# A fused attention and gated-MLP kernel: feature exponential taken straight from K and Q, some PSUM chunks emptied by VectorE, one weight block loaded later

## The chip, the cores and the metric

The kernel runs on one core of a Trainium2 chip. The metric is the device time of one execution in microseconds; before the change the median of three runs is 350.18 us (346.5 to 350.24). The core has five engines that run side by side, each with its own in-order queue: TensorE (PE, matmuls; its weight loads are shown as PEld), VectorE (DVE), ScalarE (ACT), GpSimd (POOL) and SyncE (SP, which here only issues DMAs). [...]

## What is computed

The input x is 2048 x 640 in bf16. It is layer-normed; the normed xn goes through an attention over four segments of 512 rows with a recurrent memory, and through a gated MLP, and the result is x + attention * silu(MLP). Cut to what matters:

```python
phi = lambda t: jnp.where(t > 0, t + 1.0, jnp.exp(t))
for s in range(4):                                  # segments of 512 rows, 32 heads of 20
    qs, ks, vs = q[:, :, s], k[:, :, s], v[:, :, s]
    p = softmax(einsum('bhqd,bhkd->bhqk', qs, ks) * scale + mask)
    a_dot = einsum('bhqk,bhkd->bhqd', p, vs)
    num = einsum('bhld,bhde->bhle', phi(qs), M)
    den = einsum('bhld,bhd->bhl', phi(qs), z)[..., None] + 1e-06
    o = g * num / den + (1.0 - g) * a_dot
    M = M + einsum('bhld,bhle->bhde', phi(ks), vs)
    z = z + phi(ks).sum(over l)
attn = o @ wo
mlp = (sigmoid(xn @ w_gate) * (xn @ w_up)) @ w_down   # 640 -> 1536 -> 640
out = x + attn * silu(mlp)
```

The feature map phi is t + 1 for positive t and exp(t) otherwise. It is applied to every K and Q of a segment that the memory reads or is updated with.

## The kernel before

**Tiles.** A segment is 512 rows. K and Q are kept transposed, 640 features as five chunks of 128 partitions x 512 columns in one tile (`k5`, `q5`); V is kept by rows, with a column of ones. The MLP's hidden 1536 features are 12 blocks of 128. Gate and up weights lie in three tiles each (`Wg[0..2]`, `Wu[0..2]`), four blocks of 128 columns to a tile; a load of one such tile moves 640 KB (`load_glu`, L161 to L163).

**Slots.** The scores of a segment are worked off in 20 slots (4 pairs of head groups, 5 units each). A slot begins with four or eight groups of score matmuls into the single score buffer `Sps` (L526), one softmax exponential on ScalarE over all of it (L531, into `pt`), and a mask on GpSimd (L534). The probabilities of the slot before are multiplied with V in `weigh` (L551). Between these, TensorE gets other work: V tiles, K chunks and Q chunks of the next segment, memory reads and updates, the output projection, and the MLP as filler (`gate`, `up`, `down`).

**Order.** The order of instructions on each engine is decided while the program is built. Tasks have a due time and a planned cost (`at(time, cost, fn, ...)`, L103); times are in slots, and many are multiples of R = 20/24. Tasks with a cost over 0.1 count as TensorE work (`tasks`), the others are `soft`. Each slot has two halves: up to 0.45 of the slot only `tasks` are taken, then comes `weigh`, then the rest with `tasks` and `soft`. The flag `delay` is true in the first half. The MLP's blocks fill the slots up to a common level, which is worked out from the planned costs of the tasks (L700 to L705). `later(lag, fn)` puts a soft task `lag` times R slots after the time at which the current one was due.

**Steps around the change.**
- `k_chunk` (L282), `q_chunk` (L314) and `v_tile` (L356) run five matmuls into one of three PSUM buffers that all of this work shares (`dtile`, L114), and empty it: K (L291) and V (L364) by ScalarE, Q by ScalarE in segment 0 and by VectorE in the others (`evacuate`, L276 to L280).
- `phi` (L367) handles a chunk of K or Q, 30 chunks in all: on VectorE min(t, 0) into `mn` (L370) and t + 1 in place (L371); 0.8 R later exp on ScalarE (L374); 0.5 R later the maximum of the two on VectorE (L378). For K a DMA transpose into `pkt` is issued by SP 0.7 R after that (L382).
- `k5` has one buffer, so the first K chunk of the next segment can only be emptied into it when the transposes of the segment before have read it.
- `q_bound` (L329) multiplies |Q| with the maxima of |K|: the bound that keeps the softmax exponential in range. ScalarE copies it to `cb` (L337), SP writes it to DRAM (`c_out`, L345) and reads it back as extra rows of Q (`c_in`, L353), without which a segment's scores can't start. For segments 1 to 3 it is due at 19.2 R with a planned cost of 1.12 (L660).
- At the start (`startup`, L577) nothing of the slots runs yet. Q goes to DRAM in two pieces (`stage_out`, L310), comes back in head order (`relay`, L274), the bound goes out and comes back, and SP issues all of these in program order. The second gate tile's load, `load_glu(1, 0)`, is issued after the first piece of Q (L609); the gate of block 4, the first that needs it, is the second piece of MLP work inside the slots.

Of the kernel before, what the change touches and what calls it, by code (L numbers as in the profile page):

```python
# [9 lines left out]
P = 128  # L10
# [3 lines left out]
DH = 20  # L14
# [3 lines left out]
L = 512  # L18
# [8 lines left out]
BF = mybir.dt.bfloat16  # L27
F32 = mybir.dt.float32
U16 = mybir.dt.uint16
ACT = mybir.ActivationFunctionType  # L30
ALU = mybir.AluOpType
# [24 lines left out]
R = NSLOT / 24  # L56
# [3 lines left out]
def kernel(  # L60
# [14 lines left out]
    nc = tc.nc  # L75
# [9 lines left out]
    stg = ctx.enter_context(tc.tile_pool(name="stg", bufs=1))  # L85
# [17 lines left out]
    def at(time, cost, fn, *a):  # L103
        count[0] += 1
        heapq.heappush(tasks if cost > 0.1 else soft, (time, count[0], cost, fn, a))

    seq = [0]
    delay = [False]
# [16 lines left out]
    def later(lag, fn, *a):  # L125
        at(clock[0] + lag * R, 0.0, fn, *a)
# [34 lines left out]
    def load_glu(i, which):  # L161
        w, src = ((Wg, B_w_gate), (Wu, B_w_up))[which]
        nc.sync.dma_start(w[i][:], src[:, i * L:(i + 1) * L].rearrange("(c p) n -> p c n", p=P))  # L163
# [19 lines left out]
    for i in range(8):  # L183
        va = cpool.tile([P, H, VW], BF, name=f"va{i}")
# [83 lines left out]
    def half_tile(tiles, n, half):  # L268
        return tiles[(2 * n + half) % 3]
# [3 lines left out]
        for r in range(4):  # L273
            nc.sync.dma_start(half_tile(dst, n, half)[32 * r:32 * r + DH, :, :], rows[r][:, 4 * half:4 * half + 4, :])  # L274

    def evacuate(n, dst, ps):  # L276
        if n == 0:
            nc.scalar.copy(dst, ps)
        else:
            nc.vector.tensor_copy(dst, ps)  # L280

    def k_chunk(n, c):  # L282
        s = st[n]
        if c == 0:
            s["k5"] = stg.tile([P, DC, L], BF, name="k5")
            s["kabs"] = stg.tile([P, DC], F32, name="kabs")
        ps = dtile([P, L], F32, "psk")
        for k in range(DC):
            nc.tensor.matmul(ps[:], lhsT=W["k"][:, k, c * P:(c + 1) * P], rhs=s["xnT"][:, k, :],  # L289
                             start=(k == 0), stop=(k == DC - 1))  # L290
        nc.scalar.copy(s["k5"][:, c, :], ps[:])  # L291
        if c in (2, 4) and n:
            later(0.9, stage_out, n, c // 4, Ks, KT, "k5")
        if n:
            later(0.7, k_max, n, c)
        else:
            k_max(n, c)
# [16 lines left out]
    def q_chunk(n, c):  # L314
        s = st[n]
        if c == 0:
            s["q5"] = stg.tile([P, DC, L], BF, name="q5")
            s["aq"] = stg.tile([P, DC, L], BF, name="aq")
        ps = dtile([P, L], F32, "psq")
        for k in range(DC):  # L320
            nc.tensor.matmul(ps[:], lhsT=W["q"][:, k, c * P:(c + 1) * P], rhs=s["xnT"][:, k, :],  # L321
                             start=(k == 0), stop=(k == DC - 1))
        evacuate(n, s["q5"][:, c, :], ps[:])
        nc.vector.tensor_scalar(s["aq"][:, c, :].bitcast(U16), s["q5"][:, c, :].bitcast(U16), 0x7FFF, None,
                                op0=ALU.bitwise_and)
        if c in (2, 4) and n:
            later(0.9, stage_out, n, c // 4, Qs, QT, "q5")
# [21 lines left out]
    def c_in(n, halves=(0, 1)):  # L349
        rows = Cs[n % 2].rearrange("b (g r) n -> r b g n", r=4)  # L350
        for half in halves:
            for r in range(4):
                nc.sync.dma_start(half_tile(QT, n, half)[32 * r + DH:32 * r + KR, :, :],  # L353
                                  rows[r][:, 4 * half:4 * half + 4, :])

    def v_tile(n, j, half):  # L356
        s = st[n]
        ps = dtile([P, HB], F32, "psv")
        for k in range(DC):
            nc.tensor.matmul(ps[:], lhsT=s["xnT"][:, k, j * P:(j + 1) * P],  # L360
                             rhs=W["v"][:, k, half * HB:(half + 1) * HB],
                             start=(k == 0), stop=(k == DC - 1))
        va = V[4 * (n % 2) + j]
        nc.scalar.copy(va[:, half * 16:(half + 1) * 16, 0:DH], ps[:].rearrange("p (h e) -> p h e", e=DH))  # L364


    def phi(n, src, c):  # L367
        t = st[n][src][:, c, :]
        mn = stg.tile([P, L], BF, name="mn", bufs=2)
        nc.vector.tensor_scalar(mn[:], t, 0.0, None, op0=ALU.min)  # L370
        nc.vector.tensor_scalar(t, t, 1.0, None, op0=ALU.add)  # L371

        def exp():
            nc.scalar.activation(mn[:], mn[:], ACT.Exp)  # L374
            later(0.5, rest)

        def rest():
            nc.vector.tensor_tensor(t, t, mn[:], op=ALU.max)  # L378
            if src == "k5":
                if c == 0:  # L380
                    st[n]["pkt"] = stg.tile([P, 4, D], BF, name="pkt")
                later(0.7, lambda: nc.sync.dma_start_transpose(st[n]["pkt"][:, :, c * P:(c + 1) * P], t))  # L382
        later(0.8, exp)


    def m_update(n, cs):
# [190 lines left out]
    def startup():  # L577
        warm(WARM)
        nc.gpsimd.memset(KT[0][:], 1.0)
        ln_stats(0, 0, 0, 1)  # L580
        ln_stats(0, 0, 1, 2)
        ln_norm(0, 0, 0)
        warm(10)
        ln_stats(0, 1, 0, 1)
        ln_norm(0, 0, 1)
        v_tile(0, 0, 0)
        ln_stats(0, 1, 1, 2)
        v_tile(0, 1, 0)
        ln_norm(0, 1, 0)
        v_tile(0, 0, 1)  # L590
        ln_norm(0, 1, 1)
        v_tile(0, 2, 0)
        v_tile(0, 1, 1)
        v_tile(0, 2, 1)
        v_ones(0, 4)
        make_ind()
        nc.gpsimd.memset(KT[1][:], 1.0)
        for c in range(DC):
            k_chunk(0, c)
        nc.gpsimd.memset(KT[2][:], 1.0)  # L600
        stage_out(0, 0, Ks, KT, "k5")
        for c in range(DC):
            q_chunk(0, c)
            if c == 0:
                stage_out(0, 1, Ks, KT, "k5")
                relay(0, 0, Ks, KT)
            elif c == 2:
                stage_out(0, 0, Qs, QT, "q5")
                load_glu(1, 0)  # L609
            if c < 2:  # L610
                ln_stats(1, 0, c, c + 1)
        make_bd()
        v_ones(4, 8)
        v_tile(0, 3, 0)
        v_tile(0, 3, 1)
        relay(0, 0, Qs, QT)
        q_bound(0)
        stage_out(0, 1, Qs, QT, "q5")
        c_in(0, (0,))
        load_glu(1, 1)  # L620
        ln_stats(1, 1, 0, 1)
        take(1)
        gates()
        take(1)
        ln_norm(1, 0, 0)
        ln_norm(1, 0, 1)
        take(1)
        ln_stats(1, 1, 1, 2)
        take(4)
        at(R * 2.0, 0.0, ln_norm, 1, 1, 0)  # L630
        at(R * 2.3, 0.0, ln_norm, 1, 1, 1)
        load_glu(2, 0)
        load_glu(2, 1)
        relay(0, 1, Ks, KT)
        relay(0, 1, Qs, QT)
        c_in(0, (1,))
# [6 lines left out]
    for n in range(NSEG):  # L643
        w = NSLOT * n
        m = n + 1
        if m < NSEG:
            if n:
                for p in range(2):
                    for i in range(2):
                        at(w + R * (1.4 * p + 0.7 * i - 3.4), 0.1, ln_stats, m, p, i, i + 1)  # L650
                        at(w + R * (0.4 + 1.6 * p + 0.4 * i), 0.1, ln_norm, m, p, i)
            for i in range(8):
                at(w + R * (3.5 + (0.6 * i if i < 4 else 2.5 + 0.55 * (i - 4))), 0.68, v_tile, m, i // 2, i % 2)
            for c in range(DC):
                at(w + R * (8.8 + 1.0 * c), 1.08, k_chunk, m, c)
                at(w + R * (13.8 + 1.1 * c), 1.08, q_chunk, m, c)
                if m + 1 < NSEG:
                    at(w + R * (12.8 + 0.85 * c), 0.0, phi, m, "k5", c)
                at(w + R * (18.3 + 0.8 * c), 0.0, phi, m, "q5", c)
            at(w + R * 19.2, 1.12, q_bound, m)  # L660
            if m + 1 < NSEG:
                for p in range(2):
                    at(w + R * (16.1 + p), 0.0, x_load, m + 1, p)
            if n == 0:
                for c in range(DC):
                    at(R * (2.6 + 0.8 * c), 0.0, phi, 0, "k5", c)
            for i, cs in enumerate(([0, 1, 2], [3, 4])):
                at(w + R * (10.0 + 3.2 * i), 0.75 - 0.25 * i, m_update, n, cs)
        if n >= 1:
            for j in range(4):  # L670
                at(w + R * (1.1 + 0.3 * j), 0.0, o_ready, n - 1, j)
                at(w + R * (4.0 + 0.5 * j if j < 3 else 9.6), 0.0, xr_load, n - 1, j)
            for i in range(8):
                at(w + R * (5.4 + 1.1 * i), 0.68, o_proj, n - 1, i // 2, i % 2)
                at(w + R * (3.4 + 0.85 * i), 0.25, mem_read, n, i // 2, i % 2)
# [72 lines left out]
    n = NSEG - 1  # L748
# [39 lines left out]
```

## Time and profile before

| What | Value |
|---|---|
| time, median of three runs | 350.18 us |
| the profiled execution | 350.39 us |
| its span, first to last instruction | 348.3 us |
| mean granted TensorE clock | 0.988 |
| chain that ended last | PE 79%, DVE 7%, ACT 6%, DMA 5%, issue 2% |
| softmax exponential, L531 | 80 of 1.88 us, 150.1 us |
| feature exponential, L374 | 30 of 0.63 us |
| minimum, add, maximum, L370, L371, L378 | 30 each of 0.31, 0.32 and 0.49 us |
| K and V chunks emptied by ScalarE, L291 and L364 | 20 of 0.585 us and 32 of 0.434 us |
| Q chunks emptied by VectorE, L280 | 15 of 0.687 us |

The busy share of an engine is an average over the whole span. For this kernel, in which TensorE is busy 96% of the time, a change is worth what it takes away of the time in which TensorE waits or runs at a lower clock; an engine off that path may get faster or slower without any effect. All times that follow are microseconds from the start of the span unless they are durations.

### The profile page before, as it was taken

What the parts mean: (1) busy time and instruction counts of PE and PEld (TensorE: products, weight loads), DVE (VectorE), ACT (ScalarE), POOL (GpSimd) and SP (SyncE); (2) the same over time, 40 slices, a digit from 0 to 9 for tenths busy, and PEclk for the clock granted to TensorE, in tenths of its full rate; (3) what the DMA queues carried; (4) which work ended last, traced back from release to release, by engine and by line L of the source; (5) the groups of instructions that cost most, each with busy time, mean ns of one, the idle gap of its engine ahead of it and who ended that gap; (6) DMA issues with size and microseconds to landing.
All of it is one profiled execution on the core that took longest, in us unless ns stands there. A gap on an engine that the chain in (4) does not pass through costs nothing.

```text
span 348.3 us, 8395 instructions
## 1 busy us (share of the span) xinstructions
PE 333.0 (96%) x3402; PEld 187.4 (54%) x3402; DVE 215.1 (62%) x541; ACT 233.8 (67%) x258; POOL 111.0 (32%) x157
## 2 busy tenths in 40 slices
PE   7998999899898999999989999999999999999995
PEld 7543355454455456554456446654446655544673
DVE  5365354369839456789759766685565577633455
ACT  3652589778659676667667678666678776687730
POOL 6554222222226222323214422333232322232214
PEclk9999899999989999999999999999999999999999
DMA  7955986664950641034641172123220431020032
GB/s 251 329 184 152 260 130 79 219 177 101 181 124 1 96 115 38 21 101 116 171 107 34 39 115 77 38 91 102 86 87 13 58 96 38 31 86 3 2 60 75
DMA packets 54725, 35.53 MB, mean 102 GB/s; under 512 B 28576, under 2 KB 54688, under 8 KB 54688
## 3 DMA queue, kind: packets, MB, share of 16 engines
q1 hardware_dynamic: 52480, 32.23, 37.7%
q10 hardware_dynamic: 2208, 2.79, 2.6%
q8 instruction: 26, 0.43, 0.5%
q14 instruction: 11, 0.09, 0.1%
HBM read 20.19 MB, written 8.39 MB: 82 GB/s over the span
## 4 chain that ended last, share of the span: by engine, by line
PE 79%; DVE 7%; ACT 6%; DMA 5%; issue 2%; SPq 0%; ACTq 0%; DVEq 0%
PE gp L432 13%; PE up L442 13%; PE yp L460 13%; PE Aps L551 8%; PE Sps L526 7%; PE psq L321 6%; PE sp L506 6%; PE psk L289 6%; PE psv L360 5%; ACT pt L531 3%; DMA pkt<-k 2%; DMA Cs<-cb 1%; PE dm L392 1%; PE am L414 1%; DMA Qs<-q 1%
## 5 line engine op out<-in xcount | busy, mean ns | idle before, releaser
L531 ACT ACTIVATE pt<-Sps 128x2048 bf16<-128x2048 f32 x80 | 150.1, 1876 | 20.5 <-PE Sps L526 19.8
L534 POOL TENSOR_SCALAR_AFFINE_SELECT pt<-pt 128x1024 bf16<-128x1024 bf16 (+1 forms) x80 | 75.8, 947 | 204.0 <-ACT pt L531 204.0
L432 PE MATMUL gp<-xnT,Wg 128*128 128x512 bf16 x240 | 60.7, 384 | 0.5 <-DVE hT L446 0.4
L442 PE MATMUL up<-xnT,Wu 128*128 128x512 bf16 x240 | 60.1, 381 | 0.0
L460 PE MATMUL yp<-Wd,hT 128*128 128x320 bf16 x384 | 58.7, 304 | 0.4 <-DVE hT L446 0.4
L446 DVE SCALAR_TENSOR_TENSOR hT<-tg,up 128x512 bf16<-128x512 bf16 x48 | 32.7, 681 | 32.7 <-PE up L442 28.8
L551 PEld LDWEIGHTS <-pt 128*128 128x128 bf16 x1280 | 43.2, 96 | 13.9 <-issue 1.7
L435 ACT ACTIVATE tg<-gp 128x512 bf16<-128x512 f32 x48 | 28.7, 599 | 32.6 <-PE gp L432 29.9
L551 PE MATMUL Aps<-va,pt 128*128 128x21 bf16 x1280 | 44.6, 173 | 0.2 <-DVE od L560 0.2
L460 PEld LDWEIGHTS <-hT 128*128 128x128 bf16 x384 | 35.7, 99 | 15.9 <-issue 2.2
L526 PE MATMUL Sps<-QT,KT 24*128 24x128 bf16 (+3 forms) x512 | 33.0, 302 | 6.8 <-ACT pt L531 4.9
L442 PEld LDWEIGHTS <-Wu 128*128 128x128 bf16 x240 | 21.2, 97 | 22.9 <-issue 2.3
L432 PEld LDWEIGHTS <-Wg 128*128 128x128 bf16 x240 | 21.0, 98 | 22.9 <-issue 3.9
L465 DVE SCALAR_TENSOR_TENSOR aa<-t,yp 128x320 bf16<-128x320 bf16 x32 | 15.3, 482 | 24.5 <-ACT t L463 24.4
L526 PEld LDWEIGHTS <-KT 24*128 24x128 bf16 x512 | 10.1, 92 | 34.0 <-issue 32.7
L360 PE MATMUL psv<-Wv,xnT 128*128 128x320 bf16 x160 | 26.5, 299 | 0.7 <-ACT tg L435 0.5
L463 ACT ACTIVATE t<-yp 128x320 bf16<-128x320 f32 x32 | 13.7, 438 | 18.9 <-PE yp L460 17.7
L506 PE MATMUL sp<-Wo,oT 128*128 128x320 bf16 x160 | 25.9, 300 | 0.0
L289 PE MATMUL psk<-xnT,Wk 128*128 128x512 bf16 x100 | 24.2, 379 | 1.0 <-ACT k L291 1.0
L321 PE MATMUL psq<-xnT,Wq 128*128 128x512 bf16 x100 | 24.3, 380 | 0.0
L374 ACT ACTIVATE mn<-mn 128x512 bf16<-128x512 bf16 x30 | 18.9, 633 | 7.4 <-DVE mn L370 7.4
L508 DVE SCALAR_TENSOR_TENSOR aa<-aa,sp 128x320 bf16<-128x320 bf16 x32 | 15.5, 485 | 10.6 <-PE sp L506 10.4
(73 smaller groups left out, 325.7 us busy)
## 6 DMA issues: line engine op xcount, KB each, us to landing
KT<-Ks SPq DMA_DIRECT2D x32, 80.0 KB
QT<-Qs SPq DMA_DIRECT2D x32, 80.0 KB
xr<-in_A_x_dram SPq DMA_DIRECT2D x15, 160.0 KB
out_dram<-xr SPq DMA_DIRECT2D x15, 160.0 KB
xt<-in_A_x_dram SPq DMA_DIRECT2D x6, 320.0 KB
Wg<-in_B_w_gate_dram SPq DMA_DIRECT2D x3, 640.0 KB
Wu<-in_B_w_up_dram SPq DMA_DIRECT2D x3, 640.0 KB
Wd<-in_B_w_down_dram ACTq DMA_DIRECT2D x1, 1920.0 KB
```

The source lines that it names most:

```text
L289: nc.tensor.matmul(ps[:], lhsT=W["k"][:, k, c * P:(c + 1) * P], rhs=s["xnT"][:, k, :], start=(k == 0), stop=(k == DC - 1))
L321: nc.tensor.matmul(ps[:], lhsT=W["q"][:, k, c * P:(c + 1) * P], rhs=s["xnT"][:, k, :], start=(k == 0), stop=(k == DC - 1))
L360: nc.tensor.matmul(ps[:], lhsT=s["xnT"][:, k, j * P:(j + 1) * P], rhs=W["v"][:, k, half * HB:(half + 1) * HB], start=(k == 0), stop=(k == ...
L432: nc.tensor.matmul(gp[:], lhsT=Wg[f // 4][:, k, fo:fo + P], rhs=s["xnT"][:, k, :], start=(k == 0), stop=(k == DC - 1))
L442: nc.tensor.matmul(ps[:], lhsT=Wu[f // 4][:, k, fo:fo + P], rhs=s["xnT"][:, k, :], start=(k == 0), stop=(k == DC - 1))
L446: empty(lambda: nc.vector.scalar_tensor_tensor(out=h[:], in0=tg[:], scalar=1.0, in1=ps[:], op0=ALU.add, op1=ALU.mult))
L460: nc.tensor.matmul(yp[:], lhsT=s["hT"][f][:, j * P:(j + 1) * P], rhs=W["d"][:, f, hs], start=(f == 0), stop=(f == FC - 1))
L506: nc.tensor.matmul(sp[:], lhsT=s["oT"][:, j, c, :], rhs=W["o"][:, c, hs], start=(c == 0), stop=(c == DC - 1))
L526: nc.tensor.matmul(Sps[:, r, c0:c0 + ncol], lhsT=kt[32 * r:32 * r + KR, gi, kb * P:(kb + 1) * P], rhs=qt[32 * r:32 * r + KR, gi, kb * P:L] ...
L531: nc.scalar.activation(pt[:], Sps[:], ACT.Exp, scale=SCALE)
L534: nc.gpsimd.affine_select(out=diag, in_=diag, compare_op=ALU.is_ge, fill=0.0, base=0, pattern=[[0, 4], [0, cnt], [1, P]], channel_multipli ...
L551: nc.tensor.matmul(A[:, qb, r, :], lhsT=pt[:, r, off:off + P], rhs=V[4 * (n % 2) + kb][:, 4 * g + r, :], start=first, stop=True, skip_grou ...
```

## The change

It has four parts.

1. `phi` takes the exponential straight from the K or Q chunk into a tile `ex`, at the time at which the minimum and the add stood. 0.8 R later VectorE adds 1 in place and takes max(min(ex, 1), t + 1) in one scalar_tensor_tensor. Since exp(t) is at least 1 just where t is positive, and t + 1 is then larger than 1, the result is the same function.
2. `evacuate` no longer goes by segment but by the half of the slot: with `delay` set VectorE empties the chunk, otherwise ScalarE. K chunks and V tiles use it; Q chunks stay where they were.
3. The load of the second gate tile is issued behind the first half of `c_in` of segment 0.
4. `q_bound` of segments 1 to 3 is due at 19.0 R with a planned cost of 0.6.

```diff
-    def evacuate(n, dst, ps):
-        if n == 0:
+    def evacuate(dst, ps):
+        if delay[0]:
+            nc.vector.tensor_copy(dst, ps)
+        else:
             nc.scalar.copy(dst, ps)
-        else:
-            nc.vector.tensor_copy(dst, ps)
...
-        nc.scalar.copy(s["k5"][:, c, :], ps[:])
+        evacuate(s["k5"][:, c, :], ps[:])
...
-        evacuate(n, s["q5"][:, c, :], ps[:])
+        (nc.vector.tensor_copy if n else nc.scalar.copy)(s["q5"][:, c, :], ps[:])
...
-        nc.scalar.copy(va[:, half * 16:(half + 1) * 16, 0:DH], ps[:].rearrange("p (h e) -> p h e", e=DH))
+        evacuate(va[:, half * 16:(half + 1) * 16, 0:DH], ps[:].rearrange("p (h e) -> p h e", e=DH))
...
         t = st[n][src][:, c, :]
-        mn = stg.tile([P, L], BF, name="mn", bufs=2)
-        nc.vector.tensor_scalar(mn[:], t, 0.0, None, op0=ALU.min)
-        nc.vector.tensor_scalar(t, t, 1.0, None, op0=ALU.add)
-
-        def exp():
-            nc.scalar.activation(mn[:], mn[:], ACT.Exp)
-            later(0.5, rest)
+        ex = stg.tile([P, L], BF, name="ex", bufs=2)
+        nc.scalar.activation(ex[:], t, ACT.Exp)
 
         def rest():
-            nc.vector.tensor_tensor(t, t, mn[:], op=ALU.max)
+            nc.vector.tensor_scalar(t, t, 1.0, None, op0=ALU.add)
+            nc.vector.scalar_tensor_tensor(out=t, in0=ex[:], scalar=1.0, in1=t, op0=ALU.min, op1=ALU.max)
...
-        later(0.8, exp)
+        later(0.8, rest)
...
             elif c == 2:
                 stage_out(0, 0, Qs, QT, "q5")
-                load_glu(1, 0)
...
         c_in(0, (0,))
+        load_glu(1, 0)
         load_glu(1, 1)
...
-            at(w + R * 19.2, 1.12, q_bound, m)
+            at(w + R * 19.0, 0.6, q_bound, m)
```

In the built program nine K chunks and twelve V tiles move from ScalarE to VectorE; GpSimd's order is the same, and TensorE's differs only by groups that change places around the bound and in the slots before it.

## The prediction, made before the changed kernel ran

> **What bounds the kernel now.** I read the page first, for which engine is full, then the waits by who waited for whom, then the chain in order of time without its TensorE pieces, then windows around the places that stood out, and the timeline of the worst of them. Page, rows on engines and clock:
>
> ```profile
> PE 333.0 (96%) x3402; PEld 187.4 (54%) x3402; DVE 215.1 (62%) x541; ACT 233.8 (67%) x258; POOL 111.0 (32%) x157
> ...
> PEclk9999899999989999999999999999999999999999
> ```
>
> PE is busy nearly everywhere, and two slices of 8.7 us show a lower clock. ScalarE and VectorE have room on average, so work moved between them gains nothing by itself; only time in which PE waits, or runs at half speed, can be won. Waits, engine waiting <- releaser, us in total, times, longest:
>
> ```profile
> ACT mn L374 <- DVE mn L370: 7.4, 7, 1.5
> ...
> PE Sps L526 <- ACT pt L531: 4.9, 4, 2.4
> ...
> ACT k L291 <- DMA pkt<-k: 2.5, 1, 2.5
> ...
> PE Sps L526 <- DMA QT<-Cs: 1.7, 2, 1.2
> ...
> PE psk L289 <- ACT k L291: 1.0, 1, 1.0
> ```
>
> The chain in order of time (start, us, what) names what lies behind them:
>
> ```profile
> 22.81 3.31 DMA Qs<-q
> 27.68 4.33 DMA Cs<-cb
> 32.33 2.51 DMA QT<-Cs
> ...
> 58.46 6.39 DMA pkt<-k
> ```
>
> Start-up: the first scores wait for the bound's rows, and PE's row of the up block that follows starts at 35.77 where the gate block before ended near 32.81; without the 0.40 that four score matmuls take, 2.6 us are lost. Then windows (us, PE, PEld, DVE, ACT, POOL busy, PEclk, DMA share, GB/s):
>
> ```profile
> 33.04:36.45 3.41, 1.91 (x8) 0.60 (x8) 0.00 (x0) 0.99 (x2) 0.00 (x0) 1.00 0.53 125
> 36.45:39.87 3.42, 3.42 (x16) 0.96 (x14) 0.69 (x1) 1.55 (x2) 0.68 (x1) 0.50 1.28 198
> 64.40:67.80 3.40, 2.40 (x29) 1.68 (x26) 1.40 (x3) 2.84 (x4) 0.00 (x0) 1.00 0.65 210
> 94.48:97.89 3.41, 1.39 (x16) 0.91 (x16) 1.22 (x5) 3.41 (x5) 1.10 (x1) 1.00 0.87 207
> 97.89:101.31 3.42, 3.42 (x30) 2.10 (x28) 0.93 (x2) 1.76 (x2) 1.10 (x1) 0.50 0.43 127
> ```
>
> A stretch of 3.4 us with PE busy 1.91 or 1.39 is followed by one at clock 0.50; one with 2.40 is not. Each half-speed stretch costs half of 3.42, 1.7 us. The stall in front of the second one, on the timeline (start, us, what, idle before):
>
> ```profile
> 94.05 0.63 ACT L374 ACTIVATE mn<-mn 128x512 bf16<-128x512 bf16 x1 [0.82 <-DVE mn L370]
> ...
> 94.59 1.86 ACT L531 ACTIVATE pt<-Sps 128x2048 bf16<-128x2048 f32 x1
> ...
> 96.50 0.40 PE L526 MATMUL Sps<-QT,KT 24*128 24x256 bf16 x8 [2.43 <-ACT pt L531]
> ```
>
> The scores were ready near 93.0, but ScalarE is in order: the feature exponential stood first in its queue and waited for VectorE's minimum, the softmax exponential began 1.5 us late, and the next scores waited for it, there being one score buffer. What can be won is 4.9 + 1.0 + 2.6 + 2 x 1.7 = 11.9 us.
>
> **The change, part by part.**
>
> *Exponential straight from K and Q.* 30 chunks. Removed on VectorE: minimum (0.35 for k, 0.27 for q) and maximum (0.43, 0.54); the add (0.36, 0.29) stays; added: one scalar_tensor_tensor, 128x512, all bf16 in SBUF, which before does not show. Lower bound the maximum of k, 0.43, upper bound the same operation with one operand in PSUM, 0.68 (L446); I take 0.6, nearer to the same operation. Per chunk 1.12 becomes about 0.92, in all 33.6 becomes 28 us (22.6 to 30.1). None of it is on PE's path. ScalarE's work is the same (0.63 each), but its input is now a chunk emptied slots before, so the 7.4 us of waits have no source any more. Behind those waits the softmax exponentials stood, and behind them PE's 4.9 us. What is late next: at 92.96 PE multiplies the bound and its copy cb (0.58) and, in the new order, one exponential (0.63) stand before the following softmax exponential (1.87). That is 3.2 us from the end of the bound with its semaphore, against 2.4 of PE's work (scores 0.3, down block 1.64, Aps 0.4): 0.8 us stays. Of the other three waits (0.89, 0.73, 0.83) I leave 0.2. So 4.9 becomes 1.0: -3.9.
>
> The finishing step is due 0.8 after the exponential where it was 1.3 after the minimum, so the transposes of the first K features go out earlier by half a unit of R = 20/24 slot; 80 slots in 313 us make a slot 3.9, so some 1.6 us. The last was issued at 58.46, 0.23 before the 1.9 MB load of Wd, and took 6.39; the trace has the one at 56.55 landing after 2.4. Ahead of Wd it should take about 2.4, and land some 4 us earlier than 64.86, before the K chunk that overwrites its source is ready to be emptied. That wait held ScalarE 2.5 and PE 1.0: -1.0. If the transpose is not earlier, the 1.0 stays and VectorE is blocked in ScalarE's place.
>
> *First-half chunks on VectorE.* By the new order 9 K and 12 V chunks move: ScalarE loses 9 x 0.585 + 12 x 0.434 = 10.5, VectorE gains 9 x 0.687 (L280) + 12 x 0.49 (the 128x320 rows from PSUM) = 12.1. VectorE 215.1 - 5.6 + 12.1 = 222 us, 64%; ScalarE 223. In a first half the softmax exponential of 1.9 us stands before the chunk on ScalarE; VectorE frees the buffer sooner, or later, if an hT step (0.68) is before it. Per chunk -0.2 to +0.3 on PE, of which three PSUM buffers hide most; sum -1 to +3, and I take +0.7, as VectorE is over 90% busy in a few slices.
>
> *Second gate block's load.* On SP it is moved past four Q relays, the bound's write, the second half of Q and four bound reads; its own issue is 0.49. By the trace's landing records its 640 KB (issued 23.25) landed at 30.03, the relays (issued 26.1 to 27.2) between 30.4 and 31.8 and the bound's write at 32.01. Four K relays with less before them landed 2.3 to 2.7 after issue; so the Q relays by about 29.9, the bound's write about 30.2, the reads 1.8 earlier. PE's 2.6 becomes 0.8. But the block now leaves near 31.5, and the next load of this size (33.36) took 4.5: it lands near 36.0, where gate block 4 wants it at 35.1: 0.9 back, and the up block behind it 0.6. Against that the half-speed stretch is gone if PE is idle in smaller pieces; then the up block 4 starts near 38.0 instead of 39.99. This lead meets the next limit: segment 1's last xnT transposes land at 51.6 and 52.1, the V tile that wants them started at 53.62, and DMA is full in between, so they will not be earlier. The lead shrinks to 1.7. I count start-up with its half-speed stretch at -1.7 (0 to -2.5), not at 2.6 + 1.7.
>
> *Bound earlier and cheaper in the plan.* Due 16.0 slots becomes 15.83, the second half of the slot before; planned cost 1.12 becomes 0.6, which is what five of its matmuls take (0.60 at 92.96). No instruction is added; down, gate and up blocks change places with neighbours. It puts a down block into the slot that had only bound and Aps between two score groups, which is part of the 3.9. New wait: the bound follows the last Q chunk by 1.5 to 2.0 us of PE work; emptying and absolute value take 0.69 + 0.29 and semaphores 0.2. With one hT step before them PE waits 0.4, in two segments: +0.3 on average.
>
> *The second half-speed stretch* goes with the stall before it (0.8 instead of 2.4 leaves PE over 2.40 busy): -1.7. [...]
>
> Sum: -3.9 - 1.0 + 0.7 - 1.7 + 0.3 - 1.7 = -7.3; some small waits with the same causes (PE on ScalarE's tg and on VectorE's hT, 1.3 together) I count at -0.7. So -8.0 from the profiled 350.39 (span 348.3 and 2.1 around it), 342.4; it lies 0.2 over the median 350.18, hence 342.2 in the medians' terms.
>
> **Rivals.**
> 1. *The waits move.* With the minimum gone, ScalarE's own queue (exponentials, cb, chunks of second halves) is late instead: it was busy 3.41 of 3.41 in the window at 94.48. Then half of the 3.9 and the second clock stretch stay: 342.2 + 2.0 + 1.7 = 345.9. Against it: ScalarE loses 10.5 us of work.
> [...]
> 3. *The load move gives nothing*: the block lands as late as it did behind a full queue (6.8 after issue, at 38.3), gate block 4 waits 3.2 and the lead is gone: 343.9.
> 4. *Slower*: each of the 21 chunks stands behind an hT step on VectorE (0.68) and holds its PSUM buffer, so that PE waits for it. 21 x 0.68 = 14.3 gives 342.2 - 0.7 + 14.3 = 355.8; it decides from 0.42 each. Against it: 15 Q chunks are emptied there now, and no row has PE waiting for them.
>
> **Numbers.** Forecast 0.52 (own range 339 to 344.5), rival 1 0.18, rival 2 0.12, rival 3 0.07, rival 4 0.05; 0.06 that more is won, up to all of 11.9 (338). Range 337.5 to 347: the gain of all waits at its lower end, rival 1 with a full +3 for VectorE short of its upper. A measurement here tells about 2%, 7.0 us, from no change, so faster means under 343.2: about 0.7 of the forecast, a quarter of rivals 2 and 3, a tenth of 1, all of 0.06, sum 0.50. Slower by 2% (over 357.2) only in the worst of rival 4: 0.03.
>
> **What would show it.** No ScalarE wait for VectorE before the feature exponential; PE's waits on pt near 1 us; no half-speed slice near 98; the bound's reads issued near 30.2 and the second gate block as the next wait near 35; the last K transpose landing before 61; VectorE near 222, ScalarE near 223 us. Wrong: a row of PE waiting for psk, psv on VectorE, or a scalar_tensor_tensor over 0.7.

## The result and the profile after

| | before | after |
|---|---|---|
| median of 20 runs each, taken side by side, us | 348.39 (346.29 to 351.31) | 344.28 (343.5 to 348.72) |
| ratio | | 0.9884, 95% interval [0.9858, 0.991] |
| profiled execution, us | 350.39 (span 348.3, clock 0.988) | 343.56 (span 341.8, clock 0.998) |

The change makes the kernel 1.2% faster. The forecast was 342.2 us (range 337.5 to 347). The page of the changed kernel, busy time by engine and the clock by slices:

```profile
PE 326.5 (96%) x3360; PEld 187.0 (55%) x3402; DVE 223.9 (66%) x532; ACT 225.6 (66%) x237; POOL 111.2 (33%) x157
...
PEclk9999999999999999999999999999999999999999
```

No slice has a lower clock any more, and work has moved from ScalarE to VectorE (in the records 42 of the 3402 matmuls are missing, so PE's sum is not comparable with before). The waits (engine waiting <- releaser, us in total, times, longest):

```profile
PE Sps L522 <- ACT pt L527: 4.5, 7, 1.4
...
ACT ex L370 <- DVE k L374: 3.2, 2, 2.2
...
ACT ex L370 <- DVE q L374: 2.0, 2, 1.0
...
PEld L428 <- DMA Wg<-in_B_w_gate_dram: 0.8, 1, 0.8
...
PEld L438 <- DMA Wu<-in_B_w_up_dram: 0.7, 1, 0.7
```

What the reader is to see: ScalarE's wait for the minimum (7.4) and TensorE's wait for the bound's rows (1.7) are gone, and so is ScalarE's wait for the transposes of K (2.5). But TensorE's wait for the softmax exponential is 4.5 where it was 4.9, in seven pieces instead of four, and the feature exponential waits again for VectorE, now for 5.2 us. The transfers in the chain, in order of time (start, us, what):

```profile
22.06 3.17 DMA Qs<-q
26.77 2.56 DMA Cs<-cb
31.13 5.76 DMA Wu<-in_B_w_up_dram
```

The write of the bound takes 2.56 instead of 4.33, and in place of the read of its rows the chain now runs through a weight load. On the timeline, the place where TensorE's longest wait arises (start, us, what, idle before):

```profile
50.73 0.69 DVE L442 SCALAR_TENSOR_TENSOR hT<-tg,up 128x512 bf16<-128x512 bf16 x1 [2.05 <-PE up L438]
...
51.66 0.69 DVE L374 SCALAR_TENSOR_TENSOR k<-ex,k 128x512 bf16<-128x512 bf16 x1
...
52.44 0.63 ACT L370 ACTIVATE ex<-k 128x512 bf16<-128x512 bf16 x1 [2.20 <-DVE k L374]
...
52.98 1.86 ACT L527 ACTIVATE pt<-Sps 128x2048 bf16<-128x2048 f32 x1
...
54.89 0.40 PE L522 MATMUL Sps<-QT,KT 24*128 24x128 bf16 x8 [1.39 <-ACT pt L527]
```

Read from the bottom: the scores wait 1.39 for the softmax exponential, which could have begun near 51 (the scores before it started at 50.56 and take 0.40) but stands behind a feature exponential. That one has its input, a K chunk emptied long before, but not its output: `ex` has two buffers, and the older one is held until the finishing step of its chunk has read it (51.66 to 52.35). That step stands on VectorE behind an hT step which waited 2.05 for TensorE's up block. It is before's pattern with another cause. Three more waits of 1.0 (79.93, 98.76 and 179.35) have the same releaser, and behind the last two TensorE waits 0.56 each:

```profile
98.76 0.63 ACT L370 ACTIVATE ex<-q 128x512 bf16<-128x512 bf16 x1 [1.02 <-DVE q L374]
...
101.21 0.40 PE L522 MATMUL Sps<-QT,KT 24*128 24x128 bf16 x8 [0.56 <-ACT pt L527]
```

So 1.39 + 0.56 + 0.56 = 2.5 of the 4.5 follow an exponential that waited for its buffer. The four other pieces (0.25, 0.70, 0.51 and 0.54) follow ScalarE's own work: 0.51 at 92.57 stands behind the copy of the bound and one exponential, 0.70 at 85.47 behind the copy of a down block (`t`) and one exponential.

How far the clock enters is seen over the runs. The runs of before that were taken beside the experiments, grouped by the mean granted clock of each run (one stretch of half speed, 3.41 us in the profiled before, takes 1.7 us, 0.5% of the span, from the mean), and after's 20, which were taken at another time:

| granted clock | before, runs | before, median us | after, runs | after, median us |
|---|---|---|---|---|
| 0.997 or more | 8 | 346.5 | 18 | 344.25 |
| 0.992 to 0.995 | 45 | 348.7 | 0 | |
| 0.990 or less | 20 | 350.8 | 2 | 348.5 |

At full clock the gain is some 2.2 us; the rest of the 4.1 us in the medians goes with runs at a lower mean clock, of which the changed kernel has 2 in 20 and before 65 in 73. The profiled execution of before belongs to the last group.

### The profile page after: what moved, and what is told of

Read it like the earlier page. It is cut to its first block, busy times and chain, and to the rows that moved or that the text cites. A ratio compares the mean times of both kernels' runs of the same rounds, so it can differ in the third digit from the quotient of the medians.

```text
span 341.8 us, 8316 instructions
## 1 busy us (share of the span) xinstructions
PE 326.5 (96%) x3360; PEld 187.0 (55%) x3402; DVE 223.9 (66%) x532; ACT 225.6 (66%) x237; POOL 111.2 (33%) x157
## 4 chain that ended last, share of the span: by engine, by line
PE 80%; DVE 6%; ACT 5%; DMA 4%; issue 3%; SPq 1%; POOL 1%; DVEq 0%; ACTq 0%
PE up L438 14%; PE gp L428 13%; PE yp L456 13%; PE Aps L547 8%; PE Sps L522 7%; PE psk L289 6%; PE sp L502 6%; PE psq L321 6%; PE psv L360 5%; ACT pt L527 3%; DMA Wu<-in_B_w_up_dram 2%; PE dm L388 1%; PE am L410 1%; DMA Qs<-q 1%; DVE hT L442 1%
## 5 line engine op out<-in xcount | busy, mean ns | idle before, releaser
L428 PE MATMUL gp<-xnT,Wg 128*128 128x512 bf16 x222 | 58.5, 379 | 1.8 <-DVE hT L442 0.4
L438 PE MATMUL up<-xnT,Wu 128*128 128x512 bf16 x229 | 58.9, 379 | 1.1 <-DMA Wu<-in_B_w_up_dram 0.6
L456 PE MATMUL yp<-Wd,hT 128*128 128x320 bf16 x384 | 57.1, 299 | 0.0
L522 PE MATMUL Sps<-QT,KT 24*128 24x128 bf16 (+3 forms) x512 | 31.7, 300 | 4.7 <-ACT pt L527 4.5
L289 PE MATMUL psk<-xnT,Wk 128*128 128x512 bf16 x92 | 23.5, 379 | 0.4
L502 PEld LDWEIGHTS <-oT 128*128 128x128 bf16 x160 | 14.5, 98 | 8.1 <-issue 2.0
```

What stands on the lines that cost most here:

```text
L428: nc.tensor.matmul(gp[:], lhsT=Wg[f // 4][:, k, fo:fo + P], rhs=s["xnT"][:, k, :], start=(k == 0), stop=(k == DC - 1))
L438: nc.tensor.matmul(ps[:], lhsT=Wu[f // 4][:, k, fo:fo + P], rhs=s["xnT"][:, k, :], start=(k == 0), stop=(k == DC - 1))
L456: nc.tensor.matmul(yp[:], lhsT=s["hT"][f][:, j * P:(j + 1) * P], rhs=W["d"][:, f, hs], start=(f == 0), stop=(f == FC - 1))
L502: nc.tensor.matmul(sp[:], lhsT=s["oT"][:, j, c, :], rhs=W["o"][:, c, hs], start=(c == 0), stop=(c == DC - 1))
L522: nc.tensor.matmul(Sps[:, r, c0:c0 + ncol], lhsT=kt[32 * r:32 * r + KR, gi, kb * P:(kb + 1) * P], rhs=qt[32 * r:32 * r + KR, gi, kb * P:L] ...
```

## The experiments

The theory after the result: the parts work as predicted, and what is missing is the wait for a buffer of `ex`. Its rivals: ScalarE's own queue, with exponentials back to back, holds the scores; or the worth sits elsewhere (the load, the chunks), and a lead at one place is absorbed by the next limit. Where an expectation names theories by letters, they are its own. All ratios are to runs of the kernel before that were taken beside the experiment; the line numbers of these kernels are those of before outside `phi`.

### The four parts alone

**The exponential alone** (phi_alone):

```diff
-        mn = stg.tile([P, L], BF, name="mn", bufs=2)
-        nc.vector.tensor_scalar(mn[:], t, 0.0, None, op0=ALU.min)
+        ex = stg.tile([P, L], BF, name="ex", bufs=2)
+        nc.scalar.activation(ex[:], t, ACT.Exp)
...
-            nc.vector.tensor_tensor(t, t, mn[:], op=ALU.max)
+            nc.vector.tensor_scalar(t, t, 1.0, None, op0=ALU.add)
+            nc.vector.scalar_tensor_tensor(out=t, in0=ex[:], scalar=1.0, in1=t, op0=ALU.min, op1=ALU.max)
```

> The kernel before with the new feature exponential alone. Theory A (each part is worth the TensorE waits that it removes; the exponential now waits for one of its two ex buffers instead of the minimum): ScalarE's wait for mn (7.4 us before) is gone, 4 to 6 us of waits of ex on VectorE's finishing step stand in its place, TensorE's wait on pt stays between 3.5 and 5 us, and only the last K transpose is earlier (lands before 61, no wait of the first K chunk): 1 to 2 us faster than before. Theory B (the exponential was the chief gain and the ex waits cost nothing): TensorE's wait on pt falls to some 2 us and the kernel is 3 to 4 us faster.

Measured: 345.86 us, ratio 0.9923 [0.989, 0.9956]. The wait for the minimum is gone, TensorE's wait on `pt` is 3.6 (5 pieces), and the exponentials already wait 6.6 us for VectorE. The new wait belongs to this part. The time lies between the two theories, and the clock is in it: the four runs at full clock have a median of 344.6, 1.9 less than before's 346.5 there, as theory A has it.

**The chunks alone** (evac_alone):

```diff
-        nc.scalar.copy(s["k5"][:, c, :], ps[:])
+        evacuate(s["k5"][:, c, :], ps[:])
```

and the same for `va`, with `evacuate` going by `delay`.

> The kernel before with only the first-half K chunks and V tiles emptied by VectorE. Theory A: 21 chunks move, ScalarE loses about 10 us and VectorE gains about 12, neither is on the path: within 1 us of before. The price in the prediction was +0.7 (bounds -1 to +3). Theory B (ScalarE's queue is what TensorE waits for): 2 us faster or more, with less than 3.5 us of TensorE waiting on pt.

Measured: 348.23 us, 0.9982 [0.995, 1.0013]: nothing that can be told from no change, as theory A has it. The waits of 4.9 and 7.4 stand as before.

**The load alone** (load_alone):

```diff
-                load_glu(1, 0)
...
-        load_glu(1, 1)
+        load_glu(1, 0); load_glu(1, 1)
```

> The kernel before with only the second gate block's load behind the bound's rows. Theory A: the score matmuls of slot 0 start 1.8 to 2.8 us earlier, the up block 4 starts near 37.2 where it was 39.99, no half-speed stretch near 36; the lead is kept: 2.5 us faster. Theory B (the lead meets later waits: xnT transposes, or ScalarE): the lead at 40 us is there but under 1 us of it is left at the end.

Measured: 347.72 us, 0.9966 [0.9936, 0.9997]. The first scores of slot 0 start at 32.9 without a wait, and the gate of block 4 then waits 0.77 for its weights. Less than half of the 2.5 us of theory A is there.

**The bound alone** (bound_alone):

```diff
-            at(w + R * 19.2, 1.12, q_bound, m)
+            at(w + R * 19.0, 0.6, q_bound, m)
```

> The kernel before with only the bound's due time and planned cost changed. Theory A: the slot near 94 that held only the bound and Aps gets a down block, TensorE's wait there falls from 2.4 to about 1 us, and the half-speed stretch behind it goes in those executions that had it: 1.3 us faster without the clock, up to 3 with it. Theory B (the order is only shuffled, the feature exponential's wait keeps the softmax exponential late): within 0.7 us of before.

Measured: 347.7 us, 0.9949 [0.9919, 0.9979]. The stall of 2.43 near 96 is 1.17 (the scores at 95.61), and the four runs at full clock have a median of 345.3, 1.2 less than before's: theory A.

The four gains make 0.77 + 0.18 + 0.34 + 0.51 = 1.8%, together they give 1.2%; with some 0.3% of uncertainty on each, the difference is not clear of noise. One overlap can be read: the stall near 94 to 96 was 2.43 before, 1.51 with the exponential alone, 1.17 with the bound alone and 0.51 with all. The two remove 0.92 + 1.26 = 2.18 of it singly, and 1.92 together, and a half-speed stretch that follows it can be saved only once.

### What the wait for the buffer costs

**A third buffer** (third_ex_buffer), with room made elsewhere:

```diff
-        ex = stg.tile([P, L], BF, name="ex", bufs=2)
+        ex = stg.tile([P, L], BF, name="ex", bufs=3)
...
-                dmb = stg.tile([P, HW * VW], BF, name="dmb", bufs=2)
+                dmb = stg.tile([P, HW * VW], BF, name="dmb", bufs=1)
...
-    nInd = cpool.tile([P, DC, H], F32, name="nInd")
+    nInd = cpool.tile([P, DC, H], BF, name="nInd")
```

> The changed kernel with three ex buffers in place of two (the room comes from one dmb buffer in place of two and nInd in bf16). Theory A (ScalarE's exponential waits for an ex buffer that VectorE's finishing step holds while that step stands behind other work, and this took the place of the wait for the minimum): ScalarE's 5.2 us of waits of ex on VectorE fall under 1 us, TensorE's wait on pt falls from 4.5 to 2.5 or less, 1.5 to 2.5 us faster than the changed kernel, so a ratio near 0.982 to before. Theory B (the waits on pt are ScalarE's own work, its exponentials and chunks): the ex waits go, but TensorE's wait on pt stays over 3.5 and the time is that of the changed kernel within 0.7 us.

Measured: 343.96 us, 0.9885 [0.9841, 0.9929], as the changed kernel. The waits that the missing buffer made are gone, the time is not. Its waits and, from its timeline, where the gain went:

```profile
DVE dmb L403 <- POOL Mbd L404: 7.6, 6, 2.6
...
PE Sps L526 <- ACT pt L531: 2.0, 4, 0.7
```

```profile
152.97 0.47 POOL L404 TENSOR_TENSOR Mbd<-Mbd,dmb 128x147 bf16<-128x147 bf16 x1
...
153.47 0.31 DVE L403 TENSOR_TENSOR dmb<-dm,BD 128x147 bf16<-128x147 f32 x1 [2.57 <-POOL Mbd L404]
...
153.83 1.24 PE L321 MATMUL psq<-xnT,Wq 128*128 128x512 bf16 x5 [0.80 <-DVE dmb L403]
```

The exponentials wait for nothing, and TensorE's wait on `pt` is 2.0 instead of 4.5. But the single `dmb` buffer, which made the room, lets VectorE wait 7.6 us for GpSimd, and TensorE for VectorE: its groups are 0.2 us ahead of the changed kernel at 138 us and 1.7 behind it at 152 us. Before that, a K chunk on VectorE waits 3.4 us for the transposes of K, of which the last, issued 0.2 ahead of the load of Wd, landed at 61.79. So the experiment had other causes in it beside the buffer.

**The finishing step sooner** (finish_sooner), which frees the buffer by time instead:

```diff
-        later(0.8, rest)
+        later(0.4, rest)
```

> The changed kernel with the finishing step due 0.4 R after the exponential in place of 0.8 R, buffers as they were. Theory A: the step is issued ahead of work that now stands before it on VectorE, the buffer comes free earlier, and the ex waits fall from 5.2 to some 2 us; 1 us faster than the changed kernel, if VectorE does not begin to wait for ScalarE's exponential in turn (2.5 us in the changed kernel); more than 4 us of such waits would take the gain away. Theory B: no difference beyond 0.7 us.

Measured: 342.96 us, 0.986 [0.9811, 0.9909]; TensorE's wait on `pt` is 2.0, the exponentials' wait for VectorE 0.4. The interval overlaps that of the changed kernel ([0.9858, 0.991]), but at full clock the two are apart: four runs here, none above 343.0, and 18 of the changed kernel, none below 343.5. That is theory A.

**A clean third buffer** (shared_ring): `ex` and the copy of the bound share one ring of three, where they had two and one.

```diff
-        cb = stg.tile([P, L], BF, name="cb")
+        cb = stg.tile([P, L], BF, name="ex", bufs=3)
...
-        ex = stg.tile([P, L], BF, name="ex", bufs=2)
+        ex = stg.tile([P, L], BF, name="ex", bufs=3)
```

> The changed kernel, but the exponentials' output and the bound's rows share one ring of three buffers (before, two and one of their own), so a third exponential no longer waits for the finishing step of the first, and nothing else is smaller than in the changed kernel. In third_ex_buffer the waits of the exponentials for VectorE were gone and the first exponential of 51 us was early (block at 55.0 instead of 55.9), but between 140 and 154 us it lost 1.7 us, where VectorE waited for GpSimd with the single buffer of the memory's blocks that made room there. Theory A (that single buffer took back what the third buffer gave): the lead that third_ex_buffer still had at 138 us, 0.3 us, stays to the end: 343.9 us, no wait of that kind above 2 us in all, TensorE's wait for ScalarE's exponential of the scores near 2 us instead of 4.5. Theory B (the loss of 1.7 us comes from the third buffer itself): 345 us or more at full clock, with the stalls of 141 to 154 us again. Theory C (a lead at one place is absorbed by the next): 344.2 us.

Measured: 342.23 us, 0.9807 [0.9762, 0.9851], just below the interval of the changed kernel and the lowest median of all. Five of its six runs are at full clock, none of them above 343.1, where the changed kernel's 18 begin at 343.5; no run of before beside it was at full clock, so the ratio flatters it. Its timeline where the changed kernel had the stall:

```profile
49.71 1.19 ACT L371 ACTIVATE ex<-k 128x512 bf16<-128x512 bf16 x2
50.70 0.39 PE L526 MATMUL Sps<-QT,KT 24*128 24x512 bf16 x4
...
51.21 1.88 ACT L531 ACTIVATE pt<-Sps 128x2048 bf16<-128x2048 f32 x1 [0.30 <-PE Sps L526]
...
53.57 0.40 PE L526 MATMUL Sps<-QT,KT 24*128 24x128 bf16 x8
```

The third exponential runs behind the second (x2, 49.71), the softmax exponential starts 0.5 after its scores, and the next scores, at 53.57 instead of 54.89, follow without a wait. That lead is 1.3 us at 57.6 us (the first K chunk there, 58.9 in the changed kernel), and 1.5 us at the last down blocks (315.2 against 316.8). Of TensorE's pieces on `pt`, the three behind a waiting exponential (1.39, 0.56, 0.56) are gone, here as in third_ex_buffer and finish_sooner, and the four others stay at nearly their size (0.25, 0.70, 0.57, 0.54), with one of 0.27 beside them in this kernel. The theory of the buffer stands, with a price of 1.5 us in the spans (341.8 and 340.3, both at full clock) and 2.05 us in the medians, which were not taken side by side; my expectation of 343.9 had taken the lead of third_ex_buffer for the whole gain. ScalarE's queue keeps at most the 2.3 us that TensorE still waits on `pt`.

### What the other parts carry beside it

**Without the chunks on VectorE** (without_evac, part 2 left out):

```diff
-        evacuate(s["k5"][:, c, :], ps[:])
+        nc.scalar.copy(s["k5"][:, c, :], ps[:])
```

and the same for `va`.

> The changed kernel with K chunks and V tiles emptied by ScalarE as before. Theory A (the chunks on VectorE cost what the prediction took, +0.7, because they lengthen VectorE's queue in front of the finishing steps): about 0.7 us faster than the changed kernel. Theory B (they relieve ScalarE): 0.5 to 1 us slower than the changed kernel, with more TensorE waits on ScalarE's va, k or pt.

Measured: 344.19 us, 0.9902 [0.9864, 0.994], the same as the changed kernel: part 2 moves 21 chunks and no time that these runs can tell (the interval is 0.4%, 1.3 us, to either side, which is too coarse for either theory).

**Without the load's move** (without_load, part 3 left out):

```diff
+                load_glu(1, 0)
...
-        load_glu(1, 0)
```

> The changed kernel with the second gate block's load where it was. Theory A (the load trades the wait for the bound's rows for a wait for the weights; what it wins is the clock): in executions at full clock within 0.7 us of the changed kernel, but some executions, a third or more, with a half-speed stretch of 1.7 us. Theory B (the earlier start is kept to the end): 1.5 to 2.5 us slower at full clock too.

Measured: 343.84 us, 0.9881 [0.9836, 0.9926]: no loss that these runs can tell, so not theory B. All six have a clock of 0.998 or more, so the half-speed stretches of theory A did not come either.

**With the sooner finishing step as well** (sooner_without_load):

```diff
-        later(0.8, rest)
+        later(0.4, rest)
...
+                load_glu(1, 0)
...
-        load_glu(1, 0)
```

> finish_sooner (finishing step queued 0.4 instead of 0.8 of a slot behind its exponential), with the second gate block's load left where it was before the change, ahead of the bound's rows. If the two gains add (finish_sooner 1.3 us below the changed kernel, without_load 0.4 us below it): 342.5 us. If both remove the same slack of the stretch from 49 to 62 us: 343.0 us, as finish_sooner. If the load's place matters where the steps are closer: above 343.5 us, with the second scores of slot 0 at 36 us or later.

Measured: 342.67 us, 0.9807 [0.9771, 0.9844], beside finish_sooner's 342.96: between the forecasts of 342.5 and 343.0, which six runs can't tell apart. The second scores of slot 0 do come late, but the time is not above 343.5.

Why the place of the load gives so little is on the timelines. The changed kernel:

```profile
34.97 1.25 PE L428 MATMUL gp<-xnT,Wg 128*128 128x512 bf16 x5 [0.33 <-DMA Wg<-in_B_w_gate_dram]
...
37.16 1.03 PE L438 MATMUL up<-xnT,Wu 128*128 128x512 bf16 x4 [0.61 <-DMA Wu<-in_B_w_up_dram]
```

and sooner_without_load:

```profile
33.90 0.37 PE L526 MATMUL Sps<-QT,KT 24*128 24x512 bf16 x1 [0.96 <-DMA QT<-Cs]
34.82 1.02 PE L526 MATMUL Sps<-QT,KT 24*128 24x512 bf16 x3 [0.54 <-DMA QT<-Cs]
...
53.22 0.85 PE L360 MATMUL psv<-Wv,xnT 128*128 128x320 bf16 x5 [0.85 <-DMA xnT<-xn]
```

With the load moved TensorE waits for its weights, without it for the bound's rows and later for a transpose of xn; and the wait for the rows is not in every execution: in without_load the last of them landed at 33.5 and the first scores ran from 33.0 to 34.0 without a wait of this kind, in two_parts_ring below it landed at 35.1. What differs comes ahead of the load: SP issued the first piece of Q at 22.02 in without_load and at 23.16 in two_parts_ring. Over the seven traces with the load at its old place this issue lies between 22.0 and 23.3, and TensorE waits 0 to 1.7 us before the first four score matmuls, next to nothing in two of them (evac_alone and without_load); over the seven with the load moved it lies between 21.8 and 22.4, and TensorE waits 0.1 at most. So the 1.7 of the profiled before is what an execution with a late start shows, not what every one loses. Why the start varies is not shown.

**Without the bound's new place** (without_bound, part 4 left out):

```diff
-            at(w + R * 19.0, 0.6, q_bound, m)
+            at(w + R * 19.2, 1.12, q_bound, m)
```

> The changed kernel, but the bound of the queries queued as before (due 19.2 instead of 19.0, at 1.12 instead of 0.6). If the bound's place keeps its worth beside the other parts: phi_alone showed a stall of 1.51 us at 94.1 us where the changed kernel has 0.51, so 1.0 us at full clock, and a half-speed stretch there in a part of the runs: 345.3 us, and up to 346.0 in the median with the stretches. If it is worth nothing once the exponentials need no VectorE step first: 344.3 us, TensorE's stalls as in the changed kernel.

Measured: 345.78 us, 0.9883 [0.984, 0.9926]. Its profiled span is 341.8 at clock 0.999, as the changed kernel's, and three of its six runs show a clock of 0.993 or 0.994 (346.3 to 347.1 us), where two of the changed kernel's 20 lie below 0.997. With six runs the worth of this part, between nothing and 1.5 us, stays open; what there is of it looks like clock. In its trace the stall of 1.51 is back (at 92.73), but the one at 54.89 is only 0.31 (at 54.48), so the two trade within the same span.

**Two parts and the ring** (two_parts_ring, parts 1 and 4 with shared_ring's edit, parts 2 and 3 left out):

```diff
-        evacuate(s["k5"][:, c, :], ps[:])
+        nc.scalar.copy(s["k5"][:, c, :], ps[:])
...
+                load_glu(1, 0)
...
-        load_glu(1, 0)
...
-        cb = stg.tile([P, L], BF, name="cb")
+        cb = stg.tile([P, L], BF, name="ex", bufs=3)
...
-        ex = stg.tile([P, L], BF, name="ex", bufs=2)
+        ex = stg.tile([P, L], BF, name="ex", bufs=3)
```

> Only two parts of the change, the exponential straight from the chunk and the bound queued earlier, with the ring of three buffers of shared_ring; the first half's chunks are emptied on ScalarE and the second gate block is loaded ahead of the bound's rows, as before the change. Theory A (the other two parts carry nothing): 342.2 us, as shared_ring, and no more than 0.8 us from it, with TensorE's wait for the exponential of the scores near 2 us and the block behind the third value block of 51 us at 57.6 us as there. Theory B (ScalarE, which gets back 21 chunks of 0.59 us, becomes late for the scores again): 343.5 us or more, TensorE's wait for it at 3.5 us or more.

Measured: 343.5 us, 0.9849 [0.9817, 0.9881]. That is 1.3 us over shared_ring, which was not measured beside it, so theory A misses by its own bound; but theory B falls too, as TensorE's wait on `pt` is 2.1. In the traces it is behind shared_ring by 2.3 us at the V tile behind the scores of 50.7 (53.36 against 51.03) and by 1.8 at the last down blocks: the loss is made in start-up, where TensorE waits 1.4 us for the bound's rows and then 1.0 for a transpose of xn, and some of it is won back. Part of it is this execution: the first piece of Q was issued 1.3 us later than in shared_ring (23.16 and 21.87). How much is the place of the load is not settled by the runs, since without_load and sooner_without_load lost nothing by the same edit.

## Why the prediction was right and wrong

**The exponential.** Right in that the wait for the minimum went (7.4 to none), and the softmax exponentials that stood behind it. The step that failed is: "its input is now a chunk emptied slots before, so the 7.4 us of waits have no source any more". It looked at the input alone. The output tile has two buffers, and the step that frees one is a VectorE step due 0.8 R later, behind whatever VectorE waits for. So 4.9 became 4.5 and not 1.0, and two of the prediction's own signs failed: ScalarE still waits for VectorE before the feature exponential (5.2), and TensorE's waits on `pt` are not near 1. Without the wait for the buffer (shared_ring) they come to 2.3 and the time to 342.2. The miss of 2.1 us in the time is of that size, but that shared_ring meets the forecast's 342.2 is partly chance: 2.3 is not 1.0, and the load's -1.7, the chunks' +0.7 and the bound's +0.3 did not come as counted either. The 0.8 for the place behind the bound came as 0.51 (at 92.57); the 0.70 at 85.47 has another cause, a down block's copy before the exponential. The -0.7 for small waits on `tg` and `hT` came as -0.4: 0.5 and 0.4 of the 1.3 stand as before.

**The size of the gain.** 344.28 lies inside the forecast's own range of 339 to 344.5, and some luck is in that: the largest term, -3.9, brought -0.4 in the trace, and the gain in the medians, 4.1, is half of the 8.0 that were forecast. The range was wide enough, and the sum began at an execution 2.0 above the median of 20 runs.

**K's transposes.** Right: the last was issued at 55.53 and landed at 57.94 (predicted before 61), and the waits of 2.5 and 1.0 are gone.

**The finishing step's price.** Taken at 0.6 between 0.43 and 0.68; the row says

```profile
L374 DVE SCALAR_TENSOR_TENSOR k<-ex,k x15: 691/692/1466, 44.4 to 165.6; 128x512 bf16<-128x512 bf16 x15
```

0.692 in the median (the middle one of the three), just over the upper bound. 30 x 0.09 is 2.7 us of VectorE, which came to 223.9 instead of 222 (ScalarE to 225.6 instead of 223); it lies beside TensorE, apart from lengthening the step that holds the buffer.

**Chunks on VectorE.** +0.7 was taken; without_evac shows none, within 1.3 us. No row of TensorE waiting for VectorE with `psk` or `psv` appeared, and rival 4 fell with it.

**The load.** The order of events came as described: bound written at 29.33 (30.2 predicted), the second gate block's weights the next wait at 34.97, up block 4 near 37 (38.0), and the V tile that wants the transposes of xn at 50.88 instead of 53.62, a lead of 2.7 where 1.7 was allowed. But 0.75 of that lead is ahead of the moved load, as the first piece of Q was issued at 22.06 instead of 22.81, and the transposes that were to hold the lead landed at 49.1 and 51.5 instead of 51.6 and 52.1, where the prediction had them no earlier. The term of -1.7 was mis-sized for the medians, since the wait for the bound's rows that it rests on (1.7 in the profiled before) is not in every execution: load_alone measured -0.34% [-0.64, -0.03], some 1.2 us, and left out of the whole the part costs nothing that the runs can tell. Rival 3 was right that the move gives nothing and wrong in its reason, as the block landed at 34.92, before the 36.0 that the forecast itself assumed.

**The bound.** The +0.3 for a new wait did not come.

**The clock.** Both half-speed stretches of the profiled before are gone, as predicted, and 18 of the 20 runs have a clock of 0.997 or more. But the sum took both, the second with 1.7 and the first within the start-up's 1.7, from an execution that had two, while most of before's runs (45 of 73) have a clock that fits one. That makes the predicted gain larger more than it moves the predicted time: 8.0 us were predicted from 350.39, the profiled executions differ by 6.8, the medians by 4.1. It is why "faster by over 2%" got 0.50: its bound was worked out from a median of three runs in which two were at 350.2, and 20 runs gave 348.39.

**Rival 1** put what would be left of the wait on `pt` down to ScalarE's own queue. At most the 2.3 us that stay in shared_ring are that; the rest of the 4.5 was the buffer, and no half-speed stretch stayed with it.

## What to carry to other kernels

When a step on an in-order engine is freed of waiting for its input, look for who frees its output: the number of buffers, and the engine queue in which the step that releases the oldest one stands. A third buffer, or the releasing step 0.4 R earlier, was worth 1.3 to 2 us here, beside the 2.2 that the change itself gives at full clock. An experiment that makes room for a buffer by taking another one away measures both, and the gain of a change is to be taken from many runs of before, not from one profile that has two half-speed stretches in it.

## What the runs showed of the hardware

In the profiled before the granted clock was 0.50 from 36.45 to 39.87 and from 97.89 to 101.31 (and, as in the changed kernel, in the last 1.2 us of the span, where TensorE has no work). In the 3.41 us ahead of the first two TensorE was busy for 1.91 and 1.39. In the changed kernel the stretch of that length which holds 1.04 of the 1.39 us of waiting that ended at 54.89 reads (us, then busy time of PE, PEld, DVE, ACT and POOL, clock; PE at least 2.32, as some records are missing):

```profile
53.85:57.26 3.41, 2.32 (x28) 1.38 (x29) 2.05 (x5) 3.41 (x5) 1.14 (x1) 1.00 0.47 95
```

The clock stayed full behind it (1.00 from 57.26 to 60.68). But TensorE's busy time in the stretch ahead does not settle it: in load_alone a stretch with PE at 1.65 was followed by full clock, in bound_alone one with 1.93 by half.

```profile
91.59:95.00 3.41, 1.65 (x18) 1.09 (x18) 1.01 (x4) 3.41 (x4) 1.10 (x1) 1.00 0.78 178
95.00:98.42 3.42, 3.42 (x41) 2.28 (x40) 1.41 (x3) 2.20 (x4) 1.10 (x1) 1.00 0.42 119
```

```profile
32.98:36.39 3.41, 1.93 (x8) 0.57 (x7) 0.12 (x1) 0.86 (x2) 0.00 (x0) 1.00 0.44 108
36.39:39.80 3.41, 3.41 (x10) 1.06 (x7) 0.69 (x1) 1.62 (x1) 0.68 (x1) 0.50 1.33 196
```

The weight loads took 1.09 in the first and 0.57 in the second; what decides is not shown.
